# Left keys' values of four heads in one 64x32-tile pass, and output stores on the software queue: an attention and feed-forward kernel on one Trainium2 core

## The chip, the cores and the metric

The kernel runs on one core of one Trainium2 chip. The metric is the device time of one execution in microseconds (us), as the median of some runs. A profile has a span (the time between its first and last record), which is about 1.8 us shorter than the device time of the same run. Engines are named as in the profile: PE is the matmul engine (TensorE), PEld its weight loads, DVE VectorE, ACT ScalarE, POOL GpSimd, SP the engine that does nothing here but issue transfers.

A run counts as slow when it takes over 1.5% more than the fastest of the same kernel.

## The reference

```python
# q, k, v: 8 batches x 12 heads x 448 positions x 64
def rmsnorm(x, g):
    return x / np.sqrt(np.mean(x * x, axis=-1, keepdims=True) + 1e-06) * g
q_n, k_n = rmsnorm(q, g_q), rmsnorm(k, g_k)
scores = (1.0 / np.sqrt(64)) * np.matmul(q_n, k_n.transpose(0, 1, 3, 2))
attn = np.exp(scores - np.max(scores, axis=-1, keepdims=True))
attn = attn / (np.sum(attn, axis=-1, keepdims=True) + 1e-09)
x = np.matmul(attn, v)          # then (8*448, 768): heads side by side
a, b = x @ w1, x @ w2           # 768 -> 1024, twice
out = ((a * b) @ w3) @ w_out    # (3584, 768), float32
```

The kernel multiplies `w3 @ w_out` once, at the start, so the feed-forward part (FFN below) is three products: by w1, by w2, and by `w34`.

## The kernel before

Work comes in 24 *sets* of four heads. The 448 keys of a head are three blocks of 128 *full* keys and 64 *left* keys. The probabilities of the full keys lie in `P`, those of the left keys in `Pr`, in which the 128 rows hold two heads of 64 keys each. Scores are made in units of two heads; three units make a *burst* of 24 matmuls, in tiles of 64 rows by 32 columns, eight side by side:

```python
    def qk_exp(n):
        # [cut: buffers, which keys]
        sc, z = take(2)                       # two PSUM banks
        for c0 in range(0, NP, 32):
            # [cut]
            for u in range(2):
                nc.tensor.matmul(
                    out=sc[c0 : c0 + 32, u, 0:S],
                    lhsT=qkT[u * D : (u + 1) * D, pr, 1, k0 : k0 + 32],
                    rhs=qkT[u * D : (u + 1) * D, pr, 0, 0:S],
                    start=True, stop=True, tile_position=(u * D, c0),
                )
        # [cut: the exponential on ScalarE, later]
```

The values of a set come in two halves of the head's depth (`kind` 1 and 2; kind 0 is the row sums). Each half has one PSUM bank and takes 16 matmuls in tiles of 128 by 32, four side by side. The last four of them (`j == NF`) are the left keys: `Pr` carries two heads, so half of the rows of `v` are zero for each head.

```python
    def pv_set(i, kind):
        # [cut]
        ps, z = take(1)
        for j in range(J):                    # J = 4: three full blocks, one left
            for h in range(HQ):               # four heads
                if kind:
                    w = s["v"][:, h, j, (kind - 1) * HALF : kind * HALF]
                else:
                    w = ones[:, 0 if j < NF else 1 + h // 2, :]
                nc.tensor.matmul(
                    out=ps[h * HALF : (h + 1) * HALF, :],
                    lhsT=w,
                    rhs=s["P"][:, h, j, :] if j < NF else s["Pr"][:, h % 2, :],
                    start=(j == 0), stop=(j == J - 1),
                    tile_position=(0, h * HALF),
                )
        # [cut: kind 0: reciprocal of the sums, on ScalarE]
        evac(
            z, max(clk["PE"], s["r_at"]), ["DVE"], [0.64],
            lambda e: nc.vector.tensor_tensor(
                out=xT[b][:, 2 * m + kind - 1, :], in0=ps, in1=s["r"], op=MULT
            ),
        )
```

The FFN sets fill the time between bursts (`fill`). Each takes a bank, runs 24 or 32 matmuls of 128 by 32, and is evicted by ScalarE or VectorE. One tile of eight PSUM banks (`banks`, 128 x 8 x 512) serves everything. Output tiles are stored from `ffn2`:

```python
            (nc.scalar if last and z else nc.sync).dma_start(
                out=out[r0 + t0 : r0 + t1].rearrange("(p j) n -> j p n", j=nj)[
                    j, p : p + x1 - x0, n0:n1
                ],
                in_=o_sb[x0 - c0 : x1 - c0, n0:n1],
            )
```

`nc.sync` issues on a hardware queue, which the loads and transposes of q and k use as well. The values (`v`) are loaded from `nc.gpsimd`, on the software queue. The order of all instructions is fixed when the kernel is built, by a small scheduler with an estimated clock for each engine and some dozen numbers (`KIND`, `BIAS`, `V_AHEAD` and so on).

Of the kernel before, what the change touches and what calls it, by code (L numbers as in the profile page):

```python
# [8 lines left out]
FP = mybir.dt.float32  # L9
# [9 lines left out]
def kernel(  # L19
# [34 lines left out]
    G = 3  # L54
    KIND = (2, 3, 6)
    N_PE_T = 5
# [5 lines left out]
    W_EV = 'DA'  # L62
    BIAS = 0.8
    SLACK = (0.5, 0)
    EXP_SLACK = 1.65
    WARM = 16
    WARM_GAP = 0
    PACE = 1.2
    SLACK_0 = (2.1, 0.4)
    URGE = 0.4  # L70
    AHEAD = 0.6
    LAG = 7
    UNITS = 1.3
    V_COST = 0.75
    V_AHEAD = 16
    LOAD_AT = -29
    LATE = 6
    T0 = 8.0
    LOADS = ['w1', 'q1', 'w0', 'o0', 'w2', 'v0', 'q2', 'w3', 'w4', 'w5', 'w6', 'w7', 'v1', 'o1', 'v2', 'x0', 'x1', 'v3']
    GATE = None  # L80
    GATE_T = {1: 9.5, 2: 11.0}
    AVAIL = 21.0
    LAND = {'g': 5.6, 'w1': 8.2, 'q1': 12.1, 'w0': 13.4, 'o0': 18.1, 'w2': 19.4, 'v0': 23.2, 'q2': 27.5, 'w3': 28.9, 'w4': 30.6, 'w5': 32.3, 'w6': 34.0, 'v1': 37.7, 'w7': 39.0, 'o1': 45.0, 'v2': 48.6, 'x0': 56.8, 'x1': 65.3, 'v3': 69.1, 'q3': 25.3, 'q4': 37.3, 'q5': 53.2, 'q6': 73.6}
# [37 lines left out]
    def run(e, cost, ready=0.0):  # L121
        clk[e] = max(clk[e], ready) + cost
        return clk[e]
# [6 lines left out]
    def flush_exps():  # L130
        while exps:
            one_exp()
# [168 lines left out]
    def load_w12(z):  # L301
        dst, src = ((w1s, moe_w1), (w2s, moe_w2))[z]
        for h in range(HQ):
            for half in range(2):
                nc.gpsimd.dma_start(
                    out=dst[h * HALF : (h + 1) * HALF, half::2, :],
                    in_=src.rearrange(
                        "(s h a d) f -> h a d s f", s=NQB, h=HQ, a=2, d=HALF
                    )[h, half],
                )  # L310
# [175 lines left out]


    def pv_set(i, kind):
        s = st[i]
        b, m = divmod(i, NQB)  # L490
        flush_exps()
        ps, z = take(1)
        ps = ps[:, 0:S]
        for j in range(J):
            for h in range(HQ):
                if kind:
                    w = s["v"][:, h, j, (kind - 1) * HALF : kind * HALF]
                else:
                    w = ones[:, 0 if j < NF else 1 + h // 2, :]
                nc.tensor.matmul(  # L500
                    out=ps[h * HALF : (h + 1) * HALF, :],
                    lhsT=w,
                    rhs=s["P"][:, h, j, :] if j < NF else s["Pr"][:, h % 2, :],
                    start=(j == 0),
                    stop=(j == J - 1),
                    tile_position=(0, h * HALF),
                )
        run("PE", 0.77)
        if kind == 0:
            s["r"] = att_pool.tile([128, S], FP, tag="r", name="r")  # L510
            evac(
                z, clk["PE"], ["ACT"], [0.55],
                lambda e: nc.scalar.activation(out=s["r"], in_=ps, func=AF.Ln),
            )
            nc.scalar.activation(out=s["r"], in_=s["r"], func=AF.Exp, scale=-1.0)
            s["r_at"] = run("ACT", 0.57)
            kinds_done[0] = 3 * i + 1
            return
        if b not in xT:
            xT[b] = x_pool.tile([128, CM, S], BF, tag="xT", name="xT")  # L520
        evac(
            z, max(clk["PE"], s["r_at"]), ["DVE"], [0.64],
            lambda e: nc.vector.tensor_tensor(  # L523
                out=xT[b][:, 2 * m + kind - 1, :], in0=ps, in1=s["r"], op=MULT
            ),
        )
        kinds_done[0] = 3 * i + kind + 1
        if kind == 2:
            s.clear()
            if m == NQB - 1:  # L530
                push_ffn(b)

# [80 lines left out]
    def ffn2(bp, t, nh):  # L613
# [25 lines left out]
        for z, (x0, x1) in enumerate(zip(cuts, cuts[1:])):  # L639
# [5 lines left out]
            p -= p0  # L645
            (nc.scalar if last and z else nc.sync).dma_start(
                out=out[r0 + t0 : r0 + t1].rearrange("(p j) n -> j p n", j=nj)[
# [19 lines left out]
    def fill(n):  # L667
        for _ in range(n):
            if fillers:
                fillers.pop(0)[1]()  # L670
# [72 lines left out]
    with tc.manual_schedule():  # L743
# [132 lines left out]
        def burst(m):  # L876
            flush_exps()
            for _ in range(m):
                qk_exp(units[0])

        while w34q or not fillers or clk["PE"] < LAND["x1"]:
# [43 lines left out]
        for x in range(kinds_done[0], 3 * NQ):  # L925
            i, kind = divmod(x, 3)
            last = NU * (i + 1) - 1
            at = step(last) + KIND[kind] if last >= t0 else t0 + x - kinds_done[0]
            todo.setdefault(at, []).append((i, kind))
# [3 lines left out]
            for i, kind in todo[t]  # L933
            if kind == 2 and i % NQB == NQB - 1
        ]
        room = lambda t: UNITS - V_COST * len(todo.get(t, []))
        for t in range(t0, max(todo) + 1):
# [13 lines left out]
            last = min([p for p in pushes if p >= t] or [t])  # L951
            every = sum(room(z) for z in range(t, last + 1))
            fill(int(old * room(t) / every + 0.5))
            pe_ops()
# [30 lines left out]
```

## Time and profile before

| | before |
|---|---|
| median of 3 runs (lowest to highest) | 377.24 us (376.02 to 377.59) |
| span of the profiled run | 374.3 us |
| end of PE's last matmul, from there to the end | 369.52 us, 4.81 us |
| PE busy from 80 to 340 us | 259.96 of 260 us |

The prediction shows the lines that tell what bounds it. Here are two more views. The first is the table of transfer queues, with packets, MB and the time that the packets took as a share of 16 transfer engines' span. q1 is the hardware queue, q0 the software queue, and q8 is named "instruction":

```profile
q1 hardware_dynamic: 68080, 40.61, 54.9%
q0 software_dynamic: 22560, 14.16, 26.8%
q8 instruction: 60, 0.98, 1.2%
```

The 60 packets of q8 hold 0.98 MB, 16 KB each. PE has 7,650 matmuls and as many weight loads, 15,300 in all, and 256 x 60 is 15,360: one packet seems to hold 256 of PE's instructions, at 64 bytes each.

The second is the full stage by itself (columns: length, then busy time of PE, PEld, DVE, ACT and POOL, the clock, the share of the transfer engines, GB/s):

```profile
80.00:340.00 260.00, 259.96 (x6032) 141.56 (x6024) 169.46 (x292) 215.01 (x361) 41.22 (x68) 1.00 0.82 145
```

PE is busy all the time, and starts 12,056 instructions here: 256 of them last 5.5 us.

### The profile page before, as it was taken

The page shows a single profiled execution, that of the slowest core. Times are in us where ns is not written, and L with a number is a line of the kernel's source. Part 1 is how long each engine was busy: PE and PEld are TensorE (multiplying, and loading weights), DVE is VectorE, ACT ScalarE, POOL GpSimd, SP SyncE. Part 2 cuts the span into 40 slices and gives each one's busy share as a digit, 9 for nine tenths or more (in the row PEclk, how much of TensorE's full clock was granted, in tenths as well). Part 3 has the DMA queues.
Part 4 walks back from the last instruction along what each step waited for, and adds up shares of the span by engine and source line. Part 5 has one row for each costly group of instructions (what it writes and reads, how often), then busy time and mean ns, then how long its engine had stood idle before and what let it go on. Part 6 is the DMA issues. An engine that isn't in the chain of part 4 may idle for free.

```text
span 374.3 us, 17073 instructions
## 1 busy us (share of the span) xinstructions
PE 359.2 (96%) x7650; PEld 196.1 (52%) x7650; DVE 233.9 (62%) x417; ACT 281.7 (75%) x479; POOL 80.4 (21%) x138
## 2 busy tenths in 40 slices
PE   5888899999999999999999999999999999999994
PEld 2445455555575555555555555555555555555562
DVE  4878777668878756676767566766767563322211
ACT  4877776898878898898887898888887976752231
POOL 8344545612120222022202201220202200000000
PEclk9699999999999999999999999999999999999999
DMA  8999999994999989989997799787956753014015
GB/s 186 204 229 225 214 212 232 195 158 57 209 232 179 138 166 220 189 107 137 197 198 114 129 206 224 123 156 138 224 127 79 133 123 60 2 26 108 2 25 149
DMA packets 91305, 56.43 MB, mean 151 GB/s; under 512 B 56928, under 2 KB 84640, under 8 KB 91232
## 3 DMA queue, kind: packets, MB, share of 16 engines
q1 hardware_dynamic: 68080, 40.61, 54.9%
q0 software_dynamic: 22560, 14.16, 26.8%
q8 instruction: 60, 0.98, 1.2%
q10 hardware_dynamic: 592, 0.56, 0.5%
q14 instruction: 13, 0.11, 0.1%
HBM read 46.66 MB, written 11.01 MB: 154 GB/s over the span
## 4 chain that ended last, share of the span: by engine, by line
PE 87%; DMA 10%; POOL 1%; issue 1%; DVE 0%; POOLq 0%
PE banks_ps L536 59%; PE banks_ps L500 15%; PE banks_ps L470 9%; DMA v_sb<-in_v_dram 4%; PE banks_ps L564 4%; DMA w3s<-in_moe_w_dram 4%; DMA k_sb<-in_k_dram 2%; PE banks_ps L440 1%; POOL w3s L314 0%; POOL q_sb L263 0%; PE banks_ps L552 0%; POOL g_row L753 0%; POOL g_row L752 0%; DVE o_sb L211 0%; POOL ident masks.py:199 0%
## 5 line engine op out<-in xcount | busy, mean ns | idle before, releaser
L484 ACT ACTIVATE P<-banks_ps 128x896 bf16<-128x896 f32 x144 | 123.7, 922 | 9.0 <-PE banks_ps L470 8.9
L295 POOL DMA_DIRECT2D v_sb<-in_v_dram x72 | 43.7, 618 | 193.2 <-PE banks_ps L500 164.0
L536 PE MATMUL banks_ps<-xT,w2s 128*32 128x448 bf16 x1536 | 83.3, 353 | 0.0
L536 PE MATMUL banks_ps<-xT,w1s 128*32 128x448 bf16 x1536 | 83.3, 353 | 0.0
L536 PE MATMUL banks_ps<-w34s,abT 128*32 128x384 bf16 (+2 forms) x1792 | 78.4, 326 | 0.0
L602 DVE TENSOR_TENSOR abT<-banks_ps,a_sb 128x448 bf16<-128x448 f32 x64 | 39.9, 624 | 44.0 <-PE banks_ps L536 36.1
L359 DVE TENSOR_REDUCE ssq<-sq 128x8 f32<-128x512 f32 (+1 forms) x96 | 61.6, 677 | 3.1 <-ACT sq L350 2.7
L536 PEld LDWEIGHTS <-abT 128*32 128x32 bf16 x1792 | 48.4, 97 | 26.2
L523 DVE TENSOR_TENSOR xT<-banks_ps,r 128x448 bf16<-128x448 f32 x48 | 29.8, 623 | 50.0 <-PE banks_ps L500 45.0
L536 PEld LDWEIGHTS <-w2s 128*32 128x32 bf16 x1536 | 41.3, 97 | 31.7 <-issue 1.1
L536 PEld LDWEIGHTS <-w1s 128*32 128x32 bf16 x1536 | 41.4, 97 | 31.2 <-issue 2.0
L207 ACT CAST a_sb<-banks_ps 128x448 bf16<-128x448 f32 x56 | 30.1, 537 | 31.2 <-PE banks_ps L536 30.9
L470 PE MATMUL banks_ps<-qkT 64*32 64x448 bf16 x1344 | 44.5, 360 | 1.0 <-DVE ssq L359 0.7
L500 PE MATMUL banks_ps<-P,v_sb 128*32 128x448 bf16 x576 | 36.1, 356 | 1.1 <-DMA v_sb<-in_v_dram 1.0
L207 ACT COPY o_sb<-banks_ps 128x384 f32<-128x384 f32 x44 | 20.9, 476 | 20.3 <-PE banks_ps L536 20.1
L412 DVE TENSOR_TENSOR qks<-k_sb,alpha 128x512 bf16<-128x512 f32 x48 | 32.8, 683 | 0.6 <-ACT alpha L375 0.6
L350 ACT ACTIVATE sq<-k_sb 128x512 f32<-128x512 f32 x48 | 30.5, 636 | 1.9 <-DMA k_sb<-in_k_dram 1.9
L398 DVE TENSOR_TENSOR qtmp<-q_sb,alpha 128x512 bf16<-128x512 f32 x38 | 26.1, 687 | 8.2 <-ACT alpha L375 7.6
L350 ACT ACTIVATE sq<-q_sb 128x512 f32<-128x512 f32 (+1 forms) x48 | 30.5, 634 | 0.0
L500 PEld LDWEIGHTS <-v_sb 128*32 128x32 bf16 x768 | 16.7, 96 | 25.1 <-issue 15.4
L470 PEld LDWEIGHTS <-qkT 64*32 64x32 bf16 x1344 | 14.8, 91 | 25.1 <-issue 20.2
L484 ACT ACTIVATE Pr<-banks_ps 128x896 bf16<-128x896 f32 x24 | 22.2, 925 | 4.7 <-PE banks_ps L470 4.7
(57 smaller groups left out, 264.3 us busy)
## 6 DMA issues: line engine op xcount, KB each, us to landing
out_dram<-o_sb SPq DMA_DIRECT2D x48, 192.0 KB, 3.9
q_sb<-in_q_dram SPq DMA_DIRECT2D x21, 256.0 KB, 4.8
k_sb<-in_k_dram SPq DMA_DIRECT2D x21, 256.0 KB, 5.2
q_sb<-in_q_dram SPq DMA_DIRECT2D x21, 192.0 KB, 4.6
k_sb<-in_k_dram SPq DMA_DIRECT2D x21, 192.0 KB, 5.7
v_sb<-in_v_dram POOLq DMA_DIRECT2D x24, 96.0 KB, 4.9
w3s<-in_moe_w_dram POOLq DMA_DIRECT2D x8, 256.0 KB, 11.0
w_outs<-in_moe_w_out_dram POOLq DMA_DIRECT2D x4, 384.0 KB, 9.8
```

The lines of the kernel that those rows point to most:

```text
L207: nc.scalar.copy(out=out, in_=in_)
L295: nc.gpsimd.dma_start(out=dst.rearrange("p h j d -> p h (j d)"), in_=part.rearrange("p h j d -> p h (j d)"),)
L350: nc.scalar.activation(out=s["sq", pr][0:n, t], in_=(s["q"], s["k"])[t][0:n, 2 * pr : 2 * pr + 2], func=AF.Square,)
L359: nc.vector.tensor_reduce(out=s["ssq"][0:n, t, 2 * pr : 2 * pr + 2, :], in_=s["sq", pr][0:n, t], axis=AX, op=ADD,)
L398: nc.vector.tensor_tensor(out=s["qtmp"][0:n].transpose([0, 2, 1, 3]), in0=s["q"][0:n, hs], in1=alpha[0:n, 0, hs].unsqueeze(3).broadcast_to ...
L412: nc.vector.tensor_tensor(out=s["qks", pr][:, 1].transpose([0, 2, 1, 3]), in0=s["k"][:, hs], in1=alpha[:, 1, hs].unsqueeze(3).broadcast_to ...
L470: nc.tensor.matmul(out=sc[c0 : c0 + 32, u, 0:S], lhsT=qkT[u * D : (u + 1) * D, pr, 1, k0 : k0 + 32], rhs=qkT[u * D : (u + 1) * D, pr, 0, 0:S],
L484: lambda: nc.scalar.activation(out=dst, in_=sc[:, :, 0:S], func=AF.Exp),
L500: nc.tensor.matmul(out=ps[h * HALF : (h + 1) * HALF, :], lhsT=w, rhs=s["P"][:, h, j, :] if j < NF else s["Pr"][:, h % 2, :], start=(j == 0 ...
L523: lambda e: nc.vector.tensor_tensor(out=xT[b][:, 2 * m + kind - 1, :], in0=ps, in1=s["r"], op=MULT),
L536: nc.tensor.matmul(out=ps[32 * h : 32 * h + 32, 0:n], lhsT=lhsT[:, 32 * h : 32 * h + 32], rhs=rhs, start=start, stop=stop, tile_position=( ...
L602: lambda e: nc.vector.tensor_tensor(out=abT[bp][:, fi, odd * S : (odd + 1) * S], in0=ps[:, 0:S], in1=a_sb, op=MULT,),
```

## The change

It makes the left keys' values of four heads, both halves, in one pass of eight 64x32 tiles, right behind a burst that is in that tile shape already. A row tile of 64 then holds only the keys of the head at work. Both halves of a set are now made together, in two banks. In the second bank the heads are rotated by two, so the two row tiles write different partitions of each bank; the loads of w1 and w2 are rotated to match. The second part moves all stores but the last tile's from the hardware queue to the software queue. Last, the scheduler's numbers are set anew.

```diff
-    KIND = (2, 3, 6)
+    KIND = (2, 3, 4)
-    BIAS = 0.8
-    SLACK = (0.5, 0)
-    EXP_SLACK = 1.65
+    BIAS = 0.6
+    SLACK = (0.1, 0.0)
+    EXP_SLACK = 1.05
 [cut: WARM_GAP, PACE, SLACK_0, URGE, UNITS, V_COST, HOLD, AVAIL and others]
-    V_AHEAD = 16
+    V_AHEAD = 9
-    LATE = 6
+    LATE = 4
 [cut: rows of w1 and w2 rotated for the second half]
+    def values(i):
 [cut: which set]
+        two = [take(1) for _ in range(2)]
+        for c in range(HQ):
+            for r in range(2):
+                h = 2 * r + c % 2
+                up = int(c // 2 != r)
+                nc.tensor.matmul(
+                    out=two[up][0][c * HALF : (c + 1) * HALF, 0:S],
+                    lhsT=s["v"][r * REST : (r + 1) * REST, h, NF, up * HALF : (up + 1) * HALF],
+                    rhs=s["Pr"][r * REST : (r + 1) * REST, h % 2, :],
+                    start=True, stop=False,
+                    tile_position=(r * REST, c * HALF),
+                )
+        for up, (ps, z) in enumerate(two):
 [cut: twelve full-key matmuls of 128x32 into each bank, start=False]
 [cut: the multiply by 1/sum; two of 64 partitions in the second bank]
@@ ffn2
-            (nc.scalar if last and z else nc.sync).dma_start(
+            (
+                nc.gpsimd if not last else nc.scalar if z else nc.sync
+            ).dma_start(
```

More of the change, by code (lines that the diff above doesn't have):

```diff
@@ L62 @@
     W_EV = 'DA'
-    BIAS = 0.8
-    SLACK = (0.5, 0)
-    EXP_SLACK = 1.65
+    BIAS = 0.6
+    SLACK = (0.1, 0.0)
+    EXP_SLACK = 1.05
     WARM = 16
-    WARM_GAP = 0
-    PACE = 1.2
-    SLACK_0 = (2.1, 0.4)
-    URGE = 0.4
+    WARM_GAP = 0.3
+    PACE = 1.4
+    SLACK_0 = (2.4, 0.4)
+    URGE = 0.6
     AHEAD = 0.6
     LAG = 7
-    UNITS = 1.3
-    V_COST = 0.75
-    V_AHEAD = 16
+    UNITS = 1.4
+    V_COST = 0.5
+    V_AHEAD = 9
+    HOLD = 1
+    X_PAIR = False
     LOAD_AT = -29
-    LATE = 6
+    LATE = 4
     T0 = 8.0
@@ L80 @@
     GATE = None
-    GATE_T = {1: 9.5, 2: 11.0}
-    AVAIL = 21.0
+    GATE_T = {1: 24.0, 2: 17.0}
+    AVAIL = 17.0
     LAND = {'g': 5.6, 'w1': 8.2, 'q1': 12.1, 'w0': 13.4, 'o0': 18.1, 'w2': 19.4, 'v0': 23.2, 'q2': 27.5, 'w3': 28.9, 'w4': 30.6, 'w5': 32.3, 'w6': 34.0, 'v1': 37.7, 'w7': 39.0, 'o1': 45.0, 'v2': 48.6, 'x0': 56.8, 'x1': 65.3, 'v3': 69.1, 'q3': 25.3, 'q4': 37.3, 'q5': 53.2, 'q6': 73.6}
@@ L304, in load_w12 @@
             for half in range(2):
+                p0 = (h + 2 * half) % HQ * HALF
                 nc.gpsimd.dma_start(
-                    out=dst[h * HALF : (h + 1) * HALF, half::2, :],
+                    out=dst[p0 : p0 + HALF, half::2, :],
                     in_=src.rearrange(
@@ L490, in pv_set @@
         b, m = divmod(i, NQB)
+        if kind:
+            values(i)
+            return
         flush_exps()
@@ L495, in pv_set @@
             for h in range(HQ):
-                if kind:
-                    w = s["v"][:, h, j, (kind - 1) * HALF : kind * HALF]
-                else:
-                    w = ones[:, 0 if j < NF else 1 + h // 2, :]
                 nc.tensor.matmul(
                     out=ps[h * HALF : (h + 1) * HALF, :],
-                    lhsT=w,
+                    lhsT=ones[:, 0 if j < NF else 1 + h // 2, :],
                     rhs=s["P"][:, h, j, :] if j < NF else s["Pr"][:, h % 2, :],
@@ L508, in pv_set @@
         run("PE", 0.77)
-        if kind == 0:
-            s["r"] = att_pool.tile([128, S], FP, tag="r", name="r")
-            evac(
-                z, clk["PE"], ["ACT"], [0.55],
-                lambda e: nc.scalar.activation(out=s["r"], in_=ps, func=AF.Ln),
-            )
-            nc.scalar.activation(out=s["r"], in_=s["r"], func=AF.Exp, scale=-1.0)
-            s["r_at"] = run("ACT", 0.57)
-            kinds_done[0] = 3 * i + 1
-            return
+        s["r"] = att_pool.tile([128, S], FP, tag="r", name="r")
@@ L519, in pv_set @@
+        evac(
+            z, clk["PE"], ["ACT"], [0.55],
+            lambda e: nc.scalar.activation(out=s["r"], in_=ps, func=AF.Ln),
+        )
+        nc.scalar.activation(out=s["r"], in_=s["r"], func=AF.Exp, scale=-1.0)
+        s["r_at"] = run("ACT", 0.57)
+        kinds_done[0] = 3 * i + 1
+    def values(i):
+        s = st[i]
+        b, m = divmod(i, NQB)
         if b not in xT:
             xT[b] = x_pool.tile([128, CM, S], BF, tag="xT", name="xT")
-        evac(
-            z, max(clk["PE"], s["r_at"]), ["DVE"], [0.64],
-            lambda e: nc.vector.tensor_tensor(
-                out=xT[b][:, 2 * m + kind - 1, :], in0=ps, in1=s["r"], op=MULT
-            ),
-        )
@@ L527, in pv_set @@
-        kinds_done[0] = 3 * i + kind + 1
-        if kind == 2:
-            s.clear()
-            if m == NQB - 1:
-                push_ffn(b)
+        two = [take(1) for _ in range(2)]
[7 more added lines that the diff above has]
+                    rhs=s["Pr"][r * REST : (r + 1) * REST, h % 2, :],
+                    start=True,
+                    stop=False,
+                    tile_position=(r * REST, c * HALF),
+                )
@@ new lines, in values, with scale @@
+        run("PE", 0.2)
+        for up, (ps, z) in enumerate(two):
+            for j in range(NF):
+                for c in range(HQ):
+                    h = (c + 2 * up) % HQ
+                    nc.tensor.matmul(
+                        out=ps[c * HALF : (c + 1) * HALF, 0:S],
+                        lhsT=s["v"][:, h, j, up * HALF : (up + 1) * HALF],
+                        rhs=s["P"][:, h, j, :],
+                        start=False,
+                        stop=(j == NF - 1),
+                        tile_position=(0, c * HALF),
+                    )
+            run("PE", 0.58)
+            def scale(e, ps=ps, up=up):
+                x = xT[b][:, 2 * m + up, :]
+                for p0, p1 in ((0, 64), (64, 128)) if up else ((0, 128),):
+                    r0 = (p0 + 64 * up) % 128
+                    nc.vector.tensor_tensor(
+                        out=x[p0:p1], in0=ps[p0:p1, 0:S], in1=s["r"][r0 : r0 + p1 - p0], op=MULT
+                    )
+            evac(z, max(clk["PE"], s["r_at"]), ["DVE"], [(0.64, 1.24)[up]], scale)
@@ L534, in narrow @@
+        kinds_done[0] = 3 * i + 3
+        s.clear()
+        if m == NQB - 1:
+            push_ffn(b)
     def narrow(ps, n, lhsT, rhs, start, stop):
@@ L879, in burst @@
                 qk_exp(units[0])
+            i, kind = divmod(kinds_done[0], 3)
+            if X_PAIR and kind and max(LAND.get("v%d" % i, 0), st[i]["r_at"] - 0.6) <= clk["PE"]:
+                pv_set(i, kind)
         while w34q or not fillers or clk["PE"] < LAND["x1"]:
@@ L926 @@
             i, kind = divmod(x, 3)
+            if kind == 2:
+                continue
             last = NU * (i + 1) - 1
@@ L933 @@
             for i, kind in todo[t]
-            if kind == 2 and i % NQB == NQB - 1
+            if kind and i % NQB == NQB - 1
         ]
-        room = lambda t: UNITS - V_COST * len(todo.get(t, []))
+        room = lambda t: max(0.02, UNITS - V_COST * sum(1 + kind for _, kind in todo.get(t, [])))
         for t in range(t0, max(todo) + 1):
@@ L951 @@
             last = min([p for p in pushes if p >= t] or [t])
-            every = sum(room(z) for z in range(t, last + 1))
-            fill(int(old * room(t) / every + 0.5))
+            every = max(room(t), sum(room(z) for z in range(t, last + 1)))
+            keep = HOLD if t < max(pushes) else 0
+            fill(int(max(0, old - keep) * room(t) / every + 0.5))
             pe_ops()
```

## The prediction

> **What bounds the kernel now.** I read the page from the top: the engines' shares, the slices, the chain of work that ended last.
>
> ```profile
> PE 359.2 (96%) x7650; PEld 196.1 (52%) x7650; DVE 233.9 (62%) x417; ACT 281.7 (75%) x479; POOL 80.4 (21%) x138
> ...
> PE   5888899999999999999999999999999999999994
> ...
> PEclk9699999999999999999999999999999999999999
> ...
> PE 87%; DMA 10%; POOL 1%; issue 1%; DVE 0%; POOLq 0%
> ```
>
> TensorE (PE) is busy 96% of a span of 374.3 us, and it is 87% of the chain. The first slices (9.4 us each) are not full: there the kernel waits for loads, and the second slice also had a lower clock. So there are two stages. To find where they meet I asked for busy time in stretches:
>
> ```profile
> 0.00:42.40 42.40, 32.14 (x386) 17.13 (x387) 30.80 (x67) 30.23 (x56) 22.15 (x41) 0.92 1.11 209
> 42.40:369.60 327.20, 327.07 (x7264) 179.00 (x7263) 202.68 (x351) 251.45 (x424) 58.21 (x97) 1.00 0.81 144
> ```
>
> The columns are length, then busy time of PE, PEld, DVE, ACT and POOL, the clock, the DMA share and GB/s. Before 42.4 us PE has 10.3 us of holes; from 42.4 to 369.6 us it has 0.13 us. But busy is not the same as working at the full rate, because overlapping matmuls are merged. So I looked at start-to-start times in the timeline of PE:
>
> ```profile
> 323.15 0.76 PE L470 MATMUL banks_ps<-qkT 64*32 64x448 bf16 x24
> 323.85 0.75 PE L500 MATMUL banks_ps<-P,v_sb 128*32 128x448 bf16 x12
> 324.42 0.36 PE L500 MATMUL banks_ps<-Pr,v_sb 128*32 128x448 bf16 x4
> 324.61 1.31 PE L536 MATMUL banks_ps<-xT,w1s 128*32 128x448 bf16 x24
> 325.75 1.31 PE L536 MATMUL banks_ps<-xT,w2s 128*32 128x448 bf16 x24
> 326.88 1.31 PE L536 MATMUL banks_ps<-xT,w1s 128*32 128x448 bf16 x24
> 328.12 0.76 PE L470 MATMUL banks_ps<-qkT 64*32 64x448 bf16 x24
> ```
>
> From here come my unit costs. Twenty-four FFN matmuls (six passes of four 128x32 tiles) take 325.75 - 324.61 = 1.14 us, 0.189 us a pass. The full keys' values (12, three passes) take 0.57 us, again 0.19 a pass. The left keys (Pr, 4 matmuls) take 324.61 - 324.42 = 0.19 us: one pass, though only half the rows carry keys for any head. A burst of scores (24 matmuls in 64x32 tiles, three passes of eight) takes 0.70 us, not 0.57; and the FFN set ahead of a burst takes 328.12 - 326.88 = 1.24, not 1.14. So going into a burst costs 0.10 us and coming out of it 0.13. I saw these same durations in all of 80 to 340 us; PE waits there for nobody. Time is saved only by fewer passes or fewer changes of tile shape.
>
> [...] In the score bursts each row tile has a bank of its own, [...] the changed kernel lets both row tiles write both banks, in different quadrants. [...] for a DMA issued from GpSimd [...] an issue there takes engine time, 618 ns:
>
> ```profile
> L295 POOL DMA_DIRECT2D v_sb<-in_v_dram x72 | 43.7, 618 | 193.2 <-PE banks_ps L500 164.0
> ```
>
> **The change part by part.** (1) Left keys. There are 24 sets of four heads. Before, each set has two value sets (halves of the head's depth), each with one left-key pass of four: 48 passes x 0.189 = 9.1 us (the 192 Pr,v_sb matmuls). After, eight 64x32 matmuls do both halves in one pass: 24 x 0.189 = 4.5. Saved: 4.5 us, all on the bounding engine. The full-key passes, row sums, scores and FFN are the same in number.
>
> (2) Changes of tile shape. Where the left pass follows a burst of scores directly it is already in 64x32, and the change back is one that was paid anyway. In the order of the built kernels' instructions 20 of the 24 left passes follow a burst; three early ones (loading stage) and the last stand alone. Counting changes of tile shape in the whole order I get 135 against 129; 4 of the 6 extra come after the first use of the second set's values, where PE is full: 4 x 0.11 = 0.45 us lost.
>
> (3) Where PE becomes full. PE's last hole is its wait for the second set's values, ended by a load at 40.1 us. The loads and their order are unchanged, so I keep that point. From there, passes at their unit cost sum to 314.1 us in before and 309.3 in after. That is 4.8 less, slightly over 4.5 because one transpose of w3 now runs ahead of the point, in time that was idle. Before took 369.5 - 40.1 = 329.4 for the 314.1; I carry the other 15.3 us (shape changes, the larger weights of the early stage) over.
>
> (4) Banks. A burst holds six of the eight PSUM banks and the values now want the other two together; before, one. The last of these is the bank of the FFN set just ahead of the burst, so its eviction must end within the burst's 0.70 us:
>
> ```profile
> 125.59 0.76 PE L470 MATMUL banks_ps<-qkT 64*32 64x448 bf16 x24
> 125.78 0.63 DVE L602 TENSOR_TENSOR abT<-banks_ps,a_sb 128x448 bf16<-128x448 f32 x1 [0.74 <-ACT r L515]
> ...
> 126.28 0.75 PE L500 MATMUL banks_ps<-P,v_sb 128*32 128x448 bf16 x12
> ...
> 130.72 0.76 PE L470 MATMUL banks_ps<-qkT 64*32 64x448 bf16 x24
> 130.84 0.48 ACT L207 COPY o_sb<-banks_ps 128x384 f32<-128x384 f32 x1 [1.23 <-PE banks_ps L536]
> ...
> 131.41 0.75 PE L500 MATMUL banks_ps<-P,v_sb 128*32 128x448 bf16 x12
> ```
>
> An eviction on VectorE (DVE) ends at 126.41, 0.13 after the values would start; one on ScalarE at 131.32, 0.09 before. Over the bursts of 80 to 330 us nearly all lie between -0.09 and +0.17. With a little for the signal, I estimate 0.05 us a set, 1 us in all.
>
> (5) VectorE gets 24 more multiplies (the second bank's halves are swapped, so two instructions of 64 partitions take the place of one). At the 623 ns of the xT row this is 15 us: from 233.9 to about 249, 67% of the span. It stays off the path.
>
> (6) Stores. 52 stores go from the hardware queue to the software queue: 52 x 0.62 = 32 us for GpSimd, from 80 to about 112 us of 370. Stores at the head of the hardware queue did hold up what lay behind them:
>
> ```profile
> SPq L646 <- ACT o_sb L207: 56.9, 12, 24.0
> ```
>
> But no score burst of before waits for a transposed tile after the loading stage, so this gives nothing by itself. At the end, the last tile's stores stay on the hardware queues; those of the tile before it are made some 2.6 us earlier, and should land in time.
>
> (7) The ten extra warm-up matmuls and the other numbers only move work in the loading stage or fillers between bursts: 0 us.
>
> Sum: -4.8 + 0.45 + 1.0 = -3.35 us. As the numbers were evidently set anew for this order, I allow another -0.4 for fuller early time: -3.75. 377.24 - 3.75 = 373.5 us, a ratio of 0.990.
>
> **The rivals.** First: the left pass does not run eight wide[...]. Then 24 passes x 0.189 come back and about 377.5 us results. [...] Against it: [...] scores already run eight wide. Second: PE stops for the two banks, or later because the multiplies hold them longer (2 x 0.62 us for the second) while ScalarE is busy (75% of the span, more in the full stage). At 0.2 us a set (4.8 us) the gain is gone: about 377.3 us. Against it: evictions end almost in time, as shown. Third: stores behind value loads on the software queue return output tiles late (there are three), ScalarE stops at its copy, then the exponentials, then PE: 1 to 4 us worse than my number. Against it: the value loads are also issued later, when their buffer is long free, so that queue should wait less than the 164.0 us in its row. Fourth: the loading stage holds 10.3 us of holes, and if the new order fills a third of them the time is about 370. Against it: these holes end with loads that have not changed.
>
> **Range and chances.** The first two rivals set the high side at 376.2, the fourth the low side at 370.7. Faster by 2% would need 369.7, twice the work removed, so 0.05; slower by 2% needs 384.8, a stall of 0.45 us and more in every set: 0.02. Within 2%: 0.93.
>
> **What would show it.** Right: in PE's timeline the burst and left pass together take about 0.76 us, and the full-key values start 0.13 later; PE is full from about 42 us; its last matmul ends near 366. Wrong: the left pass takes 0.38 (first rival); PE idle at the left pass, released by VectorE or ScalarE (second); ScalarE's o_sb copies released by a store (third); PE full well before 40 us (fourth). A stage before 42 us that is longer would also break it.

## The result, and the profile after

| | before | after |
|---|---|---|
| median (lowest to highest), 4 runs each | 377.41 us (376.02 to 378.13) | 389.07 us (385.79 to 392.86) |
| ratio of the fast runs | | 1.0285 (95%: 1.0202 to 1.0367), slower |
| span of the profiled run | 374.3 us | 386.1 us |
| end of PE's last matmul | 369.52 us | 378.05 us |
| from there to the end | 4.81 us | 8.07 us |

A ratio is the mean time of one kernel's fast runs over that of the other's fast runs of the same rounds, so it is not quite the ratio of the medians. The run of 392.86 us was a slow one. The prediction said 373.5 us and 370.7 to 376.2. The spans differ by 11.8 us: 8.5 us until PE's last matmul, and 3.3 us behind it.

From the page of the changed kernel: the engines, PE's slices, the two data queues, and the chain.

```profile
PE 363.4 (94%) x7660; PEld 197.0 (51%) x7660; DVE 245.1 (63%) x433; ACT 285.5 (74%) x487; POOL 109.1 (28%) x192
...
PE   5799999999979999999979999999989999999991
...
q1 hardware_dynamic: 63760, 29.99, 43.4%
q0 software_dynamic: 25184, 24.79, 35.0%
...
PE 89%; DMA 3%; issue 2%; DVE 2%; ACT 2%; DVEq 0%
```

10.6 MB have moved from q1 to q0, as intended. Past the loading stage PE's row of slices was 9 up to the last slice; now it has two 7s and an 8 in it, and the chain has 2% of "issue" (1% before), time in which the engine waited for nothing that the profile shows. The full stage:

```profile
80.00:340.00 260.00, 253.97 (x5818) 137.51 (x5817) 177.01 (x302) 212.70 (x358) 63.63 (x110) 0.99 0.81 142
```

PE is idle for 6.03 us of it, where before it was idle for 0.04. PE's waits by line say on whom (total, number of times, longest):

```profile
PE banks_ps L545 <- issue: 2.6, 1, 2.6
...
PE banks_ps L504 <- issue: 1.2, 1, 1.2
PE banks_ps L473 <- issue: 1.2, 1, 1.2
...
PE banks_ps L572 <- issue: 0.9, 1, 0.9
```

No engine and no transfer of data released PE in these four holes, 5.9 us in all. PE's timeline shows how odd they are: the second falls between the third and the fourth of four equal matmuls, and the third before the last matmul of a group.

```profile
114.25 0.36 PE L504 MATMUL banks_ps<-Pr,ones 128*32 128x448 bf16 x3
115.84 0.35 PE L504 MATMUL banks_ps<-Pr,ones 128*32 128x448 bf16 x1 [1.22 <-issue]
...
201.97 0.38 PE L545 MATMUL banks_ps<-P,v_sb 128*32 128x448 bf16 x1 [2.57 <-issue]
201.98 2.62 PE L572 MATMUL banks_ps<-xT,w1s 128*32 128x448 bf16 x24
204.05 2.22 PE L572 MATMUL banks_ps<-xT,w2s 128*32 128x448 bf16 x24
```

The longest hole has a tail: the FFN sets behind it took 2.07 and 1.89 us to the next start, not 1.14. Together that is 1.7 us more. The column of the clock, the share of its full clock that TensorE was granted, says why (0.50, third from the end):

```profile
202.20:205.50 3.30, 3.30 (x40) 1.69 (x36) 1.94 (x3) 0.87 (x2) 0.00 (x0) 0.50 1.14 216
```

In the trace's clock records TensorE was granted half of its clock for 3.41 us, from 202.16 to 205.57 us, and half of 3.41 is 1.7. Past the loading stage and before PE's last matmul such a stretch, each 3.41 us long, stands only in the four profiled runs that had an idle time of PE over 2 us there (2.57 us in this one, 2.84, 2.04 and 2.52 in three of the experiments). After idle times of up to 1.77 us there is none. So a long hole cost more than its own length.

I counted PE's instructions up to each hole in the trace's records, the sequencer's included. The holes stand at numbers 3,265, 3,521, 7,361 and 10,945. All are 193 modulo 256, so each hole lies at the end of a 16 KB block of instructions, and each ended 1.26 to 1.69 us after a packet of q8 had landed:

```
hole ends at (us)             108.55   115.84   201.97   282.65
instruction, modulo 256          193      193      193      193
packet of q8 landed at (us)   107.29   114.30   200.28   280.99
```

So I take the holes for late fetches of PE's own instructions, a packet of q8 for each 256 of them. In before nothing of the kind shows: q8 has 60 packets there too, and PE 0.04 us of idle time in the full stage, where the changed kernel has 6.03.

Past the loading stage, from PE's crossing of a block's end to the landing of its packet, before took 1.77 us in the median, 4.56 at most, and over 4 us twice. After took 1.84 in the median, 6.97 at most, and over 4 us eight times. A block lasts some 5.5 us, so the longest do not fit. The packet that began late ahead of the 2.57 us hole started 5.81 us after the crossing at 193.3 us; in those 5.81 us 234 KB of the software queue and 746 KB of the hardware queue set out. What grew is the time until the packet's start, not the packet (1.20 us in the median before, 1.10 after). That it waited among this data is my estimate from these numbers; no record says what it waited for, and the experiments test it.

The next part is the bank wait. This is the changed kernel's timeline around a left pass behind a burst:

```profile
320.96 1.31 PE L572 MATMUL banks_ps<-xT,w1s 128*32 128x448 bf16 x24
...
322.19 0.76 PE L473 MATMUL banks_ps<-qkT 64*32 64x448 bf16 x24
322.32 0.53 ACT L209 CAST a_sb<-banks_ps 128x448 bf16<-128x448 f32 x1
...
322.77 0.51 PE L532 MATMUL banks_ps<-Pr,v_sb 64*32 64x448 bf16 x8
323.21 1.32 PE L545 MATMUL banks_ps<-P,v_sb 128*32 128x448 bf16 x24
```

And the last left pass, with no burst ahead of it:

```profile
346.56 0.38 PE L532 MATMUL banks_ps<-Pr,v_sb 64*32 64x448 bf16 x8
346.87 1.32 PE L545 MATMUL banks_ps<-P,v_sb 128*32 128x448 bf16 x24
```

Alone, the left pass takes 346.87 - 346.56 = 0.31 us to the next start: one pass of eight tiles (0.189) and one change of shape (0.12). Behind the burst it takes 0.44. The 0.13 more is the second matmul of the pass, the first to need the second bank. The FFN set ahead of the burst still holds that bank: its eviction on ScalarE ends at 322.32 + 0.53 = 322.85, after the pass began at 322.77. The profile shows no idle time there: the second matmul began at 322.90, while the pass's first, begun at 322.77 and 0.35 us long, was running. Only start-to-start times show the wait. Over the 20 passes behind a burst this wait is 0.07 us where the FFN set ahead was one of `w34s` (ScalarE copies it), 0.12 to 0.22 where it was one of w1 (mostly ScalarE) and 0.14 to 0.22 where it was one of w2 (VectorE); in three places it comes as 0.23 inside the burst instead. In all it is 2.2 us in the passes and about 1 in the bursts.

The last part is the end of the program:

```profile
374.79 3.26 PE L572 MATMUL banks_ps<-w34s,abT 128*32 128x384 bf16 x76
...
376.27 1.05 POOL L684 DMA_DIRECT2D out_dram<-o_sb  x2 [1.54 <-ACT o_sb L209]
377.29 1.24 DVE L213 COPY o_sb<-banks_ps 128x512 f32<-128x512 f32 x2 [8.89 <-DMA out_dram<-o_sb]
378.00 1.39 SPq L684 DMA_DIRECT2D out_dram<-o_sb  x2
```

GpSimd issues its last stores at 376.27 us. What follows is a sequencer's record that the profile's views leave out, so I read it from the trace: a DRAIN on GpSimd begins at 376.70 and lasts 8.63 us, to 385.33; the program ends 0.8 us later. The software queue's last packet had ended at 379.64, that of SP's hardware queue at 380.66, and SP was done at 381.75. Before has that drain too, behind its last load of values: it begins at 292.81 us and lasts 5.92, and is over some 75 us before the end. What the change did is to put it behind the last stores. The release named in the third line is a decoy: the copy of the last tile begins 0.76 us ahead of the end of PE's last matmul, and in before it was 0.77 ahead (368.75 and 369.52), so the store named there delayed nothing.

Where 8.5 us until PE's last matmul come from, summed from start-to-start times from 40 us on: passes at their unit cost -4.8 us, changes of shape about +0.5, everything above these +13.2 (16.7 us against 3.45). Of the 13.2, the holes are 5.9 us, the slow sets behind the longest 1.7, the bank wait 3.2, and the transposes of the loading stage in their new order 0.6 to 0.9. Some 1.5 to 1.8 us stay unassigned. The first three terms sum to 8.9, not 8.5: the second set's values, from where I count, began at 40.12 us in before, after a wait, and at 39.62 without one in after.

### The profile page after: what moved, and what is told of

Its sections match the earlier page's. It is cut to its first block, busy times and chain, and to the rows that moved or that the text cites.

```text
span 386.1 us, 17081 instructions
## 1 busy us (share of the span) xinstructions
PE 363.4 (94%) x7660; PEld 197.0 (51%) x7660; DVE 245.1 (63%) x433; ACT 285.5 (74%) x487; POOL 109.1 (28%) x192
## 4 chain that ended last, share of the span: by engine, by line
PE 89%; DMA 3%; issue 2%; DVE 2%; ACT 2%; DVEq 0%
PE banks_ps L572 58%; PE banks_ps L473 10%; PE banks_ps L545 8%; PE banks_ps L504 5%; PE banks_ps L600 4%; DMA v_sb<-in_v_dram 3%; PE banks_ps L532 2%; PE banks_ps L716 1%; PE banks_ps L443 1%; ACT P L487 1%; DVE qks L393 1%; ACT sq L353 1%; DVE qks L415 1%; PE banks_ps L588 0%; ACT lnv L375 0%
## 5 line engine op out<-in xcount | busy, mean ns | idle before, releaser
L684 POOL DMA_DIRECT2D out_dram<-o_sb x54 | 29.4, 558 | 227.7 <-ACT o_sb L209 227.7
L572 PE MATMUL banks_ps<-xT,w2s 128*32 128x448 bf16 x1536 | 85.3, 355 | 1.0 <-issue 0.9
L572 PE MATMUL banks_ps<-xT,w1s 128*32 128x448 bf16 x1536 | 84.8, 356 | 0.0
L559 DVE TENSOR_TENSOR xT<-banks_ps,r 64x448 bf16<-64x448 f32 (+1 forms) x72 | 44.8, 622 | 44.6 <-PE banks_ps L545 43.4
L572 PEld LDWEIGHTS <-abT 128*32 128x32 bf16 x1792 | 49.6, 97 | 26.0 <-issue 2.6
L209 ACT COPY o_sb<-banks_ps 128x384 f32<-128x384 f32 x51 | 24.4, 478 | 23.6 <-PE banks_ps L572 22.1
L545 PE MATMUL banks_ps<-P,v_sb 128*32 128x448 bf16 x576 | 32.0, 354 | 2.6 <-issue 2.6
```

The costliest lines, as they stand in the source:

```text
L209: nc.scalar.copy(out=out, in_=in_)
L545: nc.tensor.matmul(out=ps[c * HALF : (c + 1) * HALF, 0:S], lhsT=s["v"][:, h, j, up * HALF : (up + 1) * HALF], rhs=s["P"][:, h, j, :], star ...
L559: nc.vector.tensor_tensor(out=x[p0:p1], in0=ps[p0:p1, 0:S], in1=s["r"][r0 : r0 + p1 - p0], op=MULT)
L572: nc.tensor.matmul(out=ps[32 * h : 32 * h + 32, 0:n], lhsT=lhsT[:, 32 * h : 32 * h + 32], rhs=rhs, start=start, stop=stop, tile_position=( ...
```

## The experiments

Before the runs I held these theories. *Stores*: the software queue's stores cost most of it, in the late fetches and the drain. *Banks*: taking two banks behind a burst makes PE wait, and costs what the left pass saves. *Numbers*: the new scheduler numbers made an order that feeds worse. A form of the first, A1, was that not the stores as such but the values' later loads (`V_AHEAD` 9) pile up with them. Except for one, the kernels ran four times each; three chips served three groups, each beside its own runs of before, whose medians were 377.31, 377.35 and 378.32 us.

### The stores put back

```diff
-            (nc.gpsimd if not last else nc.scalar if z else nc.sync).dma_start(
+            (nc.scalar if last and z else nc.sync).dma_start(
 [lines joined]
```

> The changed kernel with its output stores on the hardware queue again; all else of the change stays. Theory A (the stores on the software queue cost the time: they hold back the fetches of TensorE's own instructions, and GpSimd's drain of that queue holds the end): TensorE's holes after 80 us fall from 5.9 us to under 1, the time from TensorE's last matmul to the end of the span from 8.0 to about 4.8 us, and the time is 373 to 378 us. Theory B (the new order of work and the new numbers cost it, whatever queue the stores take): only the end gets shorter by 3.3 us, the holes stay, about 385 us.

Measured: 377.16 us (375.43 to 380.73), ratio 0.9996 (0.9931 to 1.0061), span 374.8 us. The full stage of this kernel:

```profile
80.00:340.00 260.00, 259.12 (x6008) 141.08 (x6004) 177.09 (x303) 218.61 (x367) 41.15 (x68) 1.00 0.84 145
```

PE is idle for 0.88 us, in a fetch hole of 0.56 and a wait of 0.24 for a transposed tile. So the stores are the whole slowdown, 0.029 of the time or 11 us. It also says that the rest of the change gains nothing that these runs can tell. PE's last matmul ends 0.75 us later than in before although its passes sum to 4.8 us less; the bank wait (3.4 us here), the shape changes (0.5), the early transposes (0.6 to 0.9) and these two waits (0.8) use it up: -4.8 + 5.3 to 5.6, less 0.4 for the earlier start of the second set's values (39.75 us), makes +0.1 to +0.4, and 0.3 to 0.7 us stay unassigned.

### The stores alone, on the kernel before

```diff
-            (nc.scalar if last and z else nc.sync).dma_start(
+            (nc.gpsimd if not last else nc.scalar if z else nc.sync).dma_start(
 [lines joined]
```

> The kernel before with nothing changed but the stores' queue: software queue, the last tile's stores left where they are. Theory A: TensorE gets holes of 1 to 3 us that nothing in the profile releases, and the end grows by 3.3 us: 383 to 389 us. Theory B: the end alone, 380 to 381 us.

Measured: 382.15 us (381.85 to 384.96), ratio 1.0140 (1.0082 to 1.0197), span 380.2 us. The same edit costs half as much here. There is one fetch hole, 0.58 us at 231 us, and PE's last matmul ends 2.4 us later than in before. GpSimd's drain begins at 370.53 and lasts 8.88; the end comes 8.3 us after PE's last matmul, against 4.8. The drain's share (3.5 us) is thus about that of the changed kernel (3.3), and what differs is the way until PE's last matmul, where the late fetches are.

### Small stores

All stores but the last tile's write 16 of 768 columns, in as many transfers.

```diff
-                    j, p : p + x1 - x0, n0:n1
+                    j, p : p + x1 - x0, n0 : n1 if last else n0 + 16
```

> The changed kernel, its stores on the software queue cut to 16 of 768 columns (the result is wrong on purpose; as many issues and descriptors as before, 1/48 of the bytes). If the stores' bytes hold back the instruction fetches, the holes go and the time is below 381 us; if it is [...] the order on the other queue, the holes stay and it is above 384. If the drain at the end waits for bytes, the end falls to under 6 us; if it is the queue's own, it stays at 8.

Measured: 381.14 us (380.85 to 381.76), ratio 1.0091 (1.0055 to 1.0127). One fetch hole is left, 1.41 us at 115.8 us, where the changed kernel had 5.9 us in four; the drain begins at 369.66 and lasts 8.64 (8.63 there). So the holes come mostly from the bytes in the queues, and the drain does not: it is as long when almost nothing was stored. The end took 6.8 us, neither the under 6 nor the 8 that were expected: here the drain begins 2.6 us ahead of the end of PE's last matmul, where it is 1.35 in the changed kernel.

### The left keys in 128x32 passes again

On the kernel with the stores put back, the left keys are again the fourth block of each half; all else, the two banks included, stays.

```diff
-        for c in range(HQ):
-            for r in range(2):
 [cut: the eight 64x32 matmuls]
-            for j in range(NF):
+            for j in range(J):
 [cut: start and stop]
-                        rhs=s["P"][:, h, j, :],
+                        rhs=s["P"][:, h, j, :] if j < NF else s["Pr"][:, h % 2, :],
```

> As the first of these kernels (stores on the hardware queue), with the left keys' values in two passes of four 128x32 tiles instead of one of eight 64x32; same order on all other engines. By the prediction the one pass saves 24 x 0.189 = 4.5 us, less shape changes and a stall that the changed kernel's trace puts at some 0.14 us a set: this kernel should be 1.5 to 3.5 us slower than the first of these. If the stall eats it, the two are within 0.5 us.

Measured: 378.71 us (377.06 to 381.32), ratio 1.0031 (0.9974 to 1.0088). The left keys now take 0.19 us twice, without a wait. It is 1.5 us slower than with the narrow pass, but the intervals overlap, and the profiled run had four fetch holes (2.7 us, at 193 or 194 modulo 256) although its stores were on the hardware queue. So this run shows which wait belongs to the narrow pass, but its time cannot size the pass. It shows too that the stores are not needed for a late fetch; they make it frequent.

### The values loaded early again

```diff
-    V_AHEAD = 9
+    V_AHEAD = 16
```

> The changed kernel, stores on the software queue, but the value loads asked for 16 units ahead as in the kernel before, not 9. Theory A1 (value loads pile up behind stores in GpSimd's queue, are released together with the next query and key loads, and TensorE's instruction fetches wait behind that pile): fetch delays over 4 us fall from 8 to 3 or fewer, TensorE's unreleased holes from 5.9 us to under 2, time 381 to 385 us with the drain at the end still there. Theory A2 (any stores on a second loaded queue do it, wherever the value loads are): 386 to 391 us as before this edit.

Measured: 386.44 us (386.14 to 386.99), ratio 1.0217 (1.0135 to 1.0298). Five holes, 5.6 us; nine fetches took over 4 us. A1 falls: when the values are loaded makes no difference that these runs can tell.

### The old scheduler numbers

The new structure with its stores on the hardware queue, and the kernel before's numbers. `HOLD`, a number that the kernel before does not have, stays as in the changed kernel.

```diff
-    BIAS = 0.6
-    SLACK = (0.1, 0.0)
+    BIAS = 0.8
+    SLACK = (0.5, 0)
 [cut: ten more numbers back to those of before]
```

> Stores on the hardware queue and the left keys' one pass, with the scheduler's numbers of the kernel before. If the new numbers cost what the stores do not explain (two early sets of transposes 1 us slower, fetch holes 0.8 us, a late transposed tile 0.4 us), this is 374 to 376 us, up to 3 us faster than the kernel before. If the bank wait of the left pass (3.4 us in all) is what eats the gain, it is 376 to 378, the same.

Measured: 381.34 us (379.52 to 384.70), ratio 1.0092 (1.0007 to 1.0177). That missed what I expected. In the profiled run PE waits once for 1.7 us for a multiply of VectorE ahead of a burst, and the waits in the left passes sum to 3.3 us, where they are 2.3 with the new numbers. So the old numbers bring no gain back. That the new ones serve the two-bank structure better is likely but not shown: the intervals of the two kernels (0.9931 to 1.0061 with the new numbers) overlap.

### The last quarter's stores on the hardware queue

```diff
-                nc.gpsimd if not last else nc.scalar if z else nc.sync
+                nc.gpsimd if bp < 3 else nc.scalar if last and z else nc.sync
```

> The changed kernel with only the last two batches' stores on the hardware queues. If GpSimd's drain of the software queue is what holds the end, the time from TensorE's last matmul to the end falls from 8.0 to 4.8 us, that is 3.3 us less (385 to 387 us), and the holes of the middle stay as they are. If the drain waits on something else, the end stays at 8 us.

Measured: 387.45 us (387.15 to 391.72), ratio 1.0270 (1.0184 to 1.0356). The end comes 4.4 us after PE's last matmul, as in before, and the drain, which now begins at 318.42 us and lasts 8.22, is long over by then: so it is confirmed as what held the end. But the time hardly fell: the profiled run had fetch holes of 7.7 us instead of 5.9, and eleven fetches over 4 us. The places of the holes recur: those that end at instructions 3,265, 3,521, 7,361 and 10,945 are there in this run, in the changed kernel's and in that with the values early; the last two also with the left keys in 128x32 passes, that at 3,521 with small stores, and that at 7,361, 0.56 us long, even with the stores put back. Their lengths differ (at the 7,361st 2.84, 2.57 and 0.92 us in the first three of these runs), and a gain of 3 us drowns in that.

### An FFN set between burst and left pass

On the kernel with the stores put back. This gives the bank one set's time (1.14 us) to come free.

```diff
+                if kind and (t - t0) % G == 0 and t < NQ * NU:
+                    fill(1)
```

> Stores on the hardware queue, and one FFN set between a burst of scores and the left pass, so that the bank of the FFN set ahead of the burst has 1.1 us more to be evicted; it costs a change of tile shape each way (0.23 us) in every set. If the second bank's eviction is what the left pass waits for, its second matmul no longer waits (0.00 in place of 0.07, 0.12 or 0.22 us) and a left pass takes 0.31 us to the next start in every set. If the wait is of another kind (weights, the semaphore of a second engine), it stays.

Measured in one look, whose state is not known: 386.32 us. The left pass waits 0.00 us in 18 of the 20 places, and 0.16 in two: its duration is that of the pass alone. So the bank of the FFN set ahead of the burst is what the pass waited for. The price is in the waits of PE:

```profile
PE banks_ps L572 <- DVE xT L559: 3.8, 6, 0.9
```

With one filler spent early, the w1 sets of the next batch come before VectorE has made their input. Shape changes rise from about 12 to 16.7 us as well. As a cure it is worse than the wait.

### FFN matmuls of 128x128

On the changed kernel, its stores on the software queue. A fourth of the FFN instructions do the same work, so that PE crosses a block's end half as often: 31 packets on q8 in place of 60.

```diff
-        for h in range(4):
-            nc.tensor.matmul(
-                out=ps[32 * h : 32 * h + 32, 0:n],
-                lhsT=lhsT[:, 32 * h : 32 * h + 32],
-                rhs=rhs, start=start, stop=stop,
-                tile_position=(0, 32 * h),
-            )
+        nc.tensor.matmul(out=ps[:, 0:n], lhsT=lhsT, rhs=rhs, start=start, stop=stop)
```

> The changed kernel as it is (stores on the software queue), but each four 128x32 matmuls of the FFN are one 128x128 matmul of the same columns: the same passes, about half of TensorE's instructions (some 4,000 matmuls, not 7,660), so a block of 256 instructions lasts twice as long. Theory F (the holes are late fetches of TensorE's next block of instructions): no unreleased holes after 80 us, although fetches still start late, and the end still 8 us. Rival (the holes are stalls of TensorE by DMA traffic in SBUF or PSUM, not by its instructions): holes as before, 4 to 8 us. The extra changes of shape between 128x32 and 128x128, some three a set, cost 0 to 7 us, so the time itself tells little: 383 to 392 us.

Measured: 385.24 us (383.87 to 386.05), ratio 1.0165 (1.0098 to 1.0233). The full stage of its profile:

```profile
80.00:340.00 260.00, 258.88 (x2965) 121.69 (x2964) 177.09 (x303) 215.09 (x361) 63.60 (x110) 1.00 0.77 140
```

With 5,929 instructions in 260 us a block lasts 11.2 us, twice as long, and no hole without a releaser is left, although five fetches past the loading stage still took over 4 us, the longest 7.21. PE's idle time of 1.12 us is one wait of 1.07 for a transposed tile and small ones. This is the plainest test of the fetch theory: the stores, their queue and their bytes are all there, and only the demand for instructions is halved. The time does not fall by all of the holes. The drain is still there (8.63 us from 374.87), and each change between 128x32 and 128x128 tiles costs about 0.1 us that was not paid before (the pass of row sums ahead of such a change took 86.08 - 85.79 = 0.29 us to the next start, not 0.19).

### The stores on ScalarE's hardware queue

```diff
-                nc.gpsimd if not last else nc.scalar if z else nc.sync
+                nc.scalar if not last or z else nc.sync
```

> The changed kernel with its stores on ScalarE's hardware queue. If any third loaded queue holds the instruction fetches back, the holes stay (3 us or more) and only the end is shorter; 383 to 387 us. If it is the software queue in particular, the holes fall under 1.5 us: 377 to 380 us. ScalarE spends 52 issues of some 0.5 us on it, which may cost 0 to 3 us more.

Measured: 396.27 us (395.19 to 401.53), ratio 1.0459 (1.0392 to 1.0527), the slowest of all, and a miss. There is no fetch hole, and only three fetches are over 4 us. But PE waits for ScalarE instead:

```profile
PE banks_ps L473 <- ACT r L516: 5.4, 6, 2.5
...
PE banks_ps L532 <- ACT o_sb L209: 3.4, 6, 0.6
PE banks_ps L504 <- ACT Pr L487: 2.5, 3, 1.1
```

ScalarE's 56 issues of stores took 33.0 us in all. I had not counted that they take this time just where ScalarE has evictions to do. For the fetches the run says that stores on this hardware queue, at the same points of the program, made no holes here. That the later pace of this kernel had a part in it cannot be ruled out.

### The old numbers with the stores on the software queue

> The left keys' one pass and the stores on the software queue, with the scheduler's numbers of the kernel before. Against the same kernel with stores on the hardware queue (381.3 us): if the stores' cost in the middle needs the new numbers (which place loads, transposes and value loads), this one is 3 to 6 us slower, the end alone, 384 to 387; if not, 9 to 12 us slower, 390 to 393, with holes of 4 us or more.

The edit is that of the stores alone, made to the kernel with the old scheduler numbers. Measured: 391.26 us (387.75 to 393.42), ratio 1.0328 (1.0239 to 1.0417), against 1.0092 with those numbers and the hardware queue: 0.024 of the time, about 9 us, for the stores. Its six "issue" holes sum to 6.0 us, and a seventh of 2.0 us that the profile puts down to ScalarE stands at a block's end too. The drain lasts 8.87 us. So the high cost of the stores goes with the new structure (`HOLD` included), and does not need the new numbers.

No kernel of these was clearly faster than before; the best, with the stores put back, equals it.

## Why the prediction was wrong

**Part 6, stores: the step that failed.** It said that the move "gives nothing by itself", and that the stores of the tile before the last "should land in time". They did land in time, at 379.64 us. But what the end waits for is not their landing: GpSimd's drain, now behind the last stores, took 8.63 us and cost 3.3 us. And the move is not neutral on the way. It cost 5.9 us of holes in which PE waited for its own instructions, and 1.7 us at half of the clock behind the longest. Put back, all of this goes but one hole of 0.56 us, and 11 us return. (It was 54 stores, not 52; their issues took 558 ns each, and GpSimd's 109.1 us of busy time are about the 112 predicted.) That the stores on SP had held up nothing of importance was right; the mistake was to judge a move of transfers only by the transfers that it frees, and not by those that it will collide with.

**Part 3, where PE becomes full.** It carried all time above the unit costs over, and took PE to stay full. That failed through the same holes: 6.0 us of idle PE between 80 and 340 us.

**Part 4, banks: right mechanism, wrong size.** It estimated 0.05 us a set, 1 us in all. The runs show 3.2 to 3.4 us, some 0.16 for each of the 20 passes behind a burst. The margins were read in before against the start of the full-key values, 0.70 us behind the burst's start (0.13 late behind VectorE, 0.09 early behind ScalarE), and the middle was taken. But 0.13 us of these 0.70 are the change of shape out of the burst, and the left pass has none ahead of it: it wants its banks 0.58 us behind the burst's start (322.77 - 322.19). Against that, the same evictions of before are 0.24 us late (VectorE, 126.41 - 125.59 - 0.58) and 0.02 late (ScalarE, 131.32 - 130.72 - 0.58). With 0.05 for the signal (the second matmul of the pass shown began at 322.90, the eviction ended at 322.85), this gives 0.07 and 0.29, where 0.07 to 0.22 was measured. The run with an FFN set between shows the cause.

**Parts 1 and 2, left keys and shape changes: right.** The left pass runs eight wide, 0.31 us alone; the passes' sum fell by the predicted 4.8 us, and shape changes rose by 0.35 to 0.6 us (0.45 predicted). Its two row tiles write both banks, in different partitions, and the result was correct.

**Part 5, VectorE: right.** It went to 245.1 us (about 249 predicted) and, apart from its evictions in the bank wait, PE waits for it nowhere in the full stage for more than 0.2 us.

**Part 7, the other numbers: nearly.** By the traces, and not by a run of its own, they cost 0.6 to 0.9 us in the loading stage where I had 0, and the further -0.4 us for a better-fitted order did not come.

**The rivals.** The first (the left pass does not run eight wide) is refuted. The second (a stop for two banks) named what eats the gain, at 0.16 us a set where it supposed 0.2; with the stores put back its result, about 377.3 us, is what was measured (377.16). That is partly luck: the bank wait was 3.4 us, not the 4.8 that it supposed, and smaller losses that no rival had made up the rest. The third, about stores on the software queue, foresaw a cost from the right part and by the wrong way: output buffers that come back late do not show in PE's waits in any run of the changed kernel with its stores on the software queue. The fourth (a fuller loading stage) did not happen. By the prediction's own sums the first two rivals end at 378.0 (373.5 + 4.5; it wrote 377.5) and 377.3 us, both above the 376.2 that they were said to set. And no rival had instructions or the drain, so the range was too narrow: "a stall of 0.45 us and more in every set" is not the only way to lose 2%; four holes, a stretch at half of the clock and an end did.

**What stays open.** With the stores on the software queue, the order of before has one hole of 0.6 us, and the orders with the new structure 5.6 to 8 us (1.4 with small stores, none with fewer instructions). As the holes recur at the same places of the program, the order of loads and transposes there probably makes the difference: two transposes issued one after the other precede the longest late fetch (from 192.28 us to the end of the second issue it is 6.45 us). But no run took those away by themselves. Nor do the runs tell what GpSimd does in its drain.

## What to carry to other kernels

Where a fully busy TensorE runs many small matmuls, count its own instructions as a stream too: here it took 16 KB each 5.5 us, and with the stores moved to another queue TensorE stood still for 5.9 us at the ends of four blocks. Look for holes at one place modulo 256 instructions before blaming data. Look at the granted clock behind a hole as well: here those over 2 us were followed by 3.41 us at half of it. Do not let the last transfers of a program be issued from GpSimd unless some 9 us of other work follow: where its last issues were stores, its drain took 8.63 to 8.88 us in these runs. And a saved pass is worth its time only if its results' banks are free at that moment (here the wait for them took 3.2 us of the 4.8 saved); read this from start-to-start times, since the idle columns did not show it here.
